# The last MLP chunk interleaved with the weight gradients of all tokens in an adaLN transformer block, with crossbar operands and split weight pools

## The chip, the cores and the metric

One core of one Trainium2 chip. The time is that of one execution on the device in microseconds (us), the median of several. Every kernel ran beside the kernel before on the same chip. A ratio is the mean time of one kernel's runs over the mean of the other's in the same rounds, with a 95% interval, so it is not quite the ratio of the medians quoted beside it. A class of "same" means within 2%.

In the profile's lines PE is the matrix engine (PEld its loading of weights), DVE is VectorE, ACT ScalarE, POOL GpSimd, and SPq SyncE's queue, in which transfers are issued one after the other. A pool is a region of on-chip memory that is opened and closed as a whole.

## The reference, cut to what matters

Forward and all gradients of one block: 2048 tokens, width 512, 32 heads of 16, an MLP of 1792 with squared ReLU, and scale, shift and gate vectors from a condition `c`.

```python
sa, ca, ga, sb, cb, gb = (silu(c) @ w_mod).reshape(6, D)
x1 = x + ga * (softmax_attention(layernorm(x) * (1 + ca) + sa) @ wo)
u  = (layernorm(x1) * (1 + cb) + sb) @ w1 + b1
out = x1 + gb * (relu(u)**2 @ w2 + b2)
# outputs: out, and the gradients of x, wqkv, wo, w1, b1, w2, b2, c, w_mod for a given grad_out
```

The change touches the gradients of w1 (out_4), b1 (out_5), w2 (out_6), b2 (out_7) and of `sb`, `cb`, `gb`. They need the MLP's values of all tokens with tokens on the partitions ("token-major"), while the MLP makes them with features on the partitions: something must transpose.

## The kernel before

It runs four stages: modulation; the attention forward with the MLP of each finished chunk of 512 queries worked in beside it; a weight-gradient stage; the attention backward with the last weight gradients. The weights of the MLP are loaded, scaled and transposed by the crossbar (a DMA that transposes) when the q, k and v projections are done. They lie in one pool, which takes over the memory of the projections' pools:

```python
    if (qc, g, jp) == (1, 0, 0):          # second chunk of queries begins
        bg.drain(); self.close_qkv()      # projections' pools closed
        self.open_mlp(); bg.add(self.gen_weights())
...
def open_mlp(self):
    sb = self.open_pool("mlp", bufs=1, side="right")     # w1, w2, wo, W1mT, W2gbT, wogaT
    self.mk = self.open_pool("mlpk", bufs=1, side="right")
def gen_weights(self):
    nc.sync.dma_start(wo...); nc.sync.dma_start(w1...); nc.sync.dma_start(w2...)
    ... # wo *= gate
    nc.sync.dma_start_transpose(self.wogaT..., wo...)
    ... # w2 *= gate
    nc.sync.dma_start_transpose(self.W2gbT..., w2...)    # 128 x 7168, 1792 KB
```

The same SyncE queue carries, for each piece of 512 tokens of each group of four heads, the store of q or k and a small crossbar transpose:

```python
def gen_fm(self, ps, t, g, s0, eng="vector"):     # one piece of q or k
    ... 4 matmuls -> pt
    ev = eb.tile([P, 512], BF16, name="ev_fm")    # 3 buffers
    nc.vector.tensor_scalar(ev[:], pt[:], bc, None, ALU.add)
    nc.sync.dma_start((self.QTq_d, self.KTq_d)[t][g, :, s0:s0 + 512], ev[:])
    tm = eb.tile([P, 4, 4, 32], BF16, name="ev_tm")
    nc.sync.dma_start_transpose(tm[:]..., ev[:])
```

The weight-gradient stage transposes on PE, block by block, after the last MLP chunk:

```python
for ft in range(FT):                              # 14 blocks of 128 features
    ... # load rT_f, duT_f; square rT_f
    for (srcT, dst, eng) in ((aT_f, a_blk, "act"), (duT_f, du_blk, "dve")):
        ... # 16 PE transposes each, evicted by ACT or DVE
    ... # 16 matmuls -> g2 (w2 gradient), 1 float32 accumulation
    ... # 64 narrow matmuls -> g4 (w1 gradient)
```

The softmax here doesn't subtract the row's maximum and nothing guards it: scores larger than these inputs give would overflow.

Of the kernel before, what the change touches and what calls it, by code (L numbers as in the profile page):

```python
# [8 lines left out]
BF16 = mybir.dt.bfloat16  # L9
# [9 lines left out]
P = 128  # L19
# [53 lines left out]
class K:  # L73
# [29 lines left out]
    def build(self, ctx: ExitStack):  # L103
# [22 lines left out]
        phases = [self.phase0, self.phase_fwd, self.phase45, self.phase5, self.phase6]  # L126
# [136 lines left out]
    def phase_fwd(self):  # L263
# [18 lines left out]
        pup = self.open_pool("fwp", bufs=4)  # L282
        stp = self.open_pool("fwst", bufs=2, space=PSUM)
        accp = self.open_pool("fwacc", bufs=1, space=PSUM)
        self.mps = self.open_pool("mps", bufs=3, space=PSUM)
# [71 lines left out]
        bg.drain()  # L357
        self.close_mlp()
        for name in ("mps", "fwacc", "fwst", "fwp", "fwk", "fw"):
            self.close_pool(name)  # L360

# [151 lines left out]
    def open_mlp(self):  # L513
        nc, io = self.nc, self.io
        D, F, DT, FT, SC, NQ = self.D, self.F, self.DT, self.FT, self.SC, self.NQ
        sb = self.open_pool("mlp", bufs=1, side="right")
        self.mk = self.open_pool("mlpk", bufs=1, side="right")
        self.w1 = sb.tile([P, DT, F], BF16, name="w1")
        self.w2 = sb.tile([P, FT, D], BF16, name="w2")
        self.wo = sb.tile([P, DT, D], BF16, name="wo3")  # L520
        self.W1mT = sb.tile([P, DT, FT, P], BF16, name="W1mT")
        self.W2gbT = sb.tile([P, FT, DT, P], BF16, name="W2gbT")
        self.wogaT = sb.tile([P, DT, DT, P], BF16, name="wogaT")
        self.bias1 = sb.tile([P, FT], F32, name="bias1")
        self.b2gb_b = sb.tile([1, D], BF16, name="b2gb_b")
        self.mhalf = sb.tile([P, 4], F32, name="mhalf")
        nc.vector.memset(self.mhalf[:], -0.5)
        self.db1_part = sb.tile([P, FT, SC], F32, name="db1_part")
        nc.vector.memset(self.db1_part[:], 0.0)
        self.dOpads = [sb.tile([P, NQ, 4, 32], BF16, name=f"dOpad{i}") for i in range(2)]  # L530
        for t in self.dOpads:
            nc.gpsimd.memset(t[:], 0.0)

    def close_mlp(self):
        nc = self.nc
        nc.vector.tensor_reduce(self.db1[:], self.db1_part[:], axis=AX.X, op=ALU.add)
        db1_b = self.mk.tile([P, self.FT], BF16, name="db1_b")
        nc.vector.tensor_copy(db1_b[:], self.db1[:])
        with nc.allow_non_contiguous_dma(reason="column-layout store"):
            nc.sync.dma_start(self.io["out_5"].rearrange("(t p) -> p t", p=P), db1_b[:])  # L540
        self.close_pool("mlpk")
        self.close_pool("mlp")
# [50 lines left out]
    def gen_mlp(self, sc, O_b):  # L593
# [36 lines left out]
        rT = mk.tile([P, FT, 512], BF16, name="rT")  # L630
# [12 lines left out]
        nc.gpsimd.dma_start(self.rT_d.rearrange("ft p s -> p ft s")[:, :, s0:s0 + 512], rT[:])  # L643
        yield ("wait", 1)
        for k in range(4):
# [8 lines left out]
            nc.gpsimd.dma_start(out_v[:, k, :], o[:])  # L654
        duT = mk.tile([P, FT, 512], BF16, name="auT")
# [7 lines left out]
        nc.gpsimd.dma_start(self.duT_d.rearrange("ft p s -> p ft s")[:, :, s0:s0 + 512], duT[:])  # L663
        yield ("wait", 1)
        todo = []
        for k in range(4):
# [18 lines left out]
            todo.append((k, dxT))  # L685
            if k:
# [66 lines left out]

    def gen_4b(self, sb2, lb, ob, accps, ps, trps):
        tc, nc, pp, io = self.tc, self.nc, self.pp, self.io
        S, D, F, H, ST, DT, FT, SC = self.S, self.D, self.F, self.H, self.ST, self.DT, self.FT, self.SC
        g_v = io["grad_out"][0].rearrange("(st p) d -> p st d", p=P)
        xh2_v = self.xhat2_d.rearrange("(st p) d -> p st d", p=P)
        db1 = self.db1
        g_tm = sb2.tile([P, ST, D], BF16, name="g_tm")  # L760
        nc.sync.dma_start(g_tm[:], g_v)
        xh2 = sb2.tile([P, ST, D], BF16, name="xh2")
        nc.gpsimd.dma_start(xh2[:], xh2_v)
        w1_v = io["B_w1"].rearrange("(kt p) f -> p kt f", p=P)
        b2_b = sb2.tile([P, D], BF16, name="b2_b")
        nc.sync.dma_start(b2_b[:], io["B_b2"].rearrange("(o d) -> o d", o=1).to_broadcast([P, D]))
        csg_ps = ps.tile([P, 512], F32, name="g2ps")
        for st in range(ST):
            nc.tensor.matmul(csg_ps[:, :D], lhsT=self.ones_b[:], rhs=g_tm[:, st, :], start=(st == 0), stop=(st == ST - 1))
        csg = sb2.tile([P, D], F32, name="csg")  # L770
        nc.vector.tensor_copy(csg[:], csg_ps[:, :D])
        db2 = sb2.tile([P, D], BF16, name="db2")
        nc.vector.tensor_tensor(db2[:], csg[:], self.mod_row(5), ALU.mult)
        nc.sync.dma_start(io["out_7"].rearrange("(o d) -> o d", o=1), db2[0:1, :])
        db1_bc = sb2.tile([P, F], F32, name="db1_bc")
        acc_cb = sb2.tile([P, DT, P], F32, name="acc_cb")
        nc.vector.memset(acc_cb[:], 0.0)
        opcb_b = self.opcbT[:].unsqueeze(2).to_broadcast([P, DT, P])
        sbT_b = self.mod_col(3).unsqueeze(2).to_broadcast([P, DT, P])
        dgb_ps = accps.tile([P, 512], F32, name="dgb_ps")  # L780
        dw1_v = io["out_4"].rearrange("(kt p) f -> p kt f", p=P)
        yield
        for ft in range(FT):
            rT_f = lb.tile([P, S], BF16, name="rT_f")
            duT_f = lb.tile([P, S], BF16, name="duT_f")
            nc.sync.dma_start(rT_f[:], self.rT_d[ft])
            nc.gpsimd.dma_start(duT_f[:], self.duT_d[ft])
            w2_blk = lb.tile([P, D], BF16, name="w2_blk")
            w1_blk = lb.tile([P, DT, P], BF16, name="w1_blk")
            with nc.allow_non_contiguous_dma(reason="256B runs"):  # L790
                nc.sync.dma_start(w1_blk[:], w1_v[:, :, ft * P:(ft + 1) * P])
            nc.gpsimd.dma_start(w2_blk[:], io["B_w2"][ft * P:(ft + 1) * P, :])
            aT_f = rT_f
            nc.scalar.activation(aT_f[:], rT_f[:], ACT.Square)
            a_blk = lb.tile([P, ST, P], BF16, name="a_blk")
            du_blk = lb.tile([P, ST, P], BF16, name="du_blk")
            for (srcT, dst, eng) in ((aT_f, a_blk, "act"), (duT_f, du_blk, "dve")):
                for s0 in range(0, ST, 8):
                    n = min(8, ST - s0)
                    pt = trps.tile([P, 8 * P], BF16, name="trps")  # L800
                    for k in range(n):
                        nc.tensor.transpose(pt[:, k * P:(k + 1) * P], srcT[:, (s0 + k) * P:(s0 + k + 1) * P], self.ident[:])
                    dv = dst[:, s0:s0 + n, :].rearrange("p s f -> p (s f)")
                    if eng == "act":
                        nc.scalar.copy(dv, pt[:, :n * P])
                    else:
                        nc.vector.tensor_copy(dv, pt[:, :n * P])
            g2 = ps.tile([P, 512], F32, name="g2ps")
            for st in range(ST):
                nc.tensor.matmul(g2[:, :D], lhsT=a_blk[:, st, :], rhs=g_tm[:, st, :], start=(st == 0), stop=(st == ST - 1))  # L810
            dw2 = ob.tile([P, D], BF16, name="dw2")
            nc.vector.tensor_tensor(dw2[:], g2[:, :D], self.mod_row(5), ALU.mult)
            nc.sync.dma_start(io["out_6"][ft * P:(ft + 1) * P, :], dw2[:])
            tmp = ob.tile([P, D], F32, name="g2w2")
            nc.vector.tensor_tensor(tmp[:], g2[:, :D], w2_blk[:], ALU.mult)
            nc.tensor.matmul(dgb_ps[:, :D], lhsT=self.ones_f[:], rhs=tmp[:], start=(ft == 0), stop=(ft == FT - 1))
            yield
            g4 = ps.tile([P, DT, P], F32, name="g4ps")
            for kt in range(DT):
                for st in range(ST):  # L820
                    nc.tensor.matmul(g4[:, kt, :], lhsT=xh2[:, st, kt * P:(kt + 1) * P], rhs=du_blk[:, st, :],
                                     start=(st == 0), stop=(st == ST - 1))
            diag = ob.tile([P, P], F32, name="diag")
            nc.vector.tensor_scalar(diag[:], self.ident_f[:], db1[:, ft:ft + 1], None, ALU.mult)
            csb_ps = ps.tile([P, P], F32, name="csbps")
            nc.tensor.matmul(csb_ps[:], lhsT=self.ones_f[:], rhs=diag[:], start=True, stop=True)
            csb = db1_bc[:, ft * P:(ft + 1) * P]
# [473 lines left out]
```

## Time and profile before

| what | us |
|---|---|
| median (3 runs, 3136.89 to 3143.05) | 3139.95 |
| profiled execution | 3141.7 |
| attention forward, first to last exponential | 104.3 to 1131.5 |
| from there to the first score matmul of the backward, the stretch that the change rebuilds | 326.3 |
| attention backward and the rest | 1683.9 |

The prediction below shows the stretch.

```profile
127.76 0.53 SPq L445 DMA_DIRECT2D QTq_d<-ev_fm  x1
...
136.57 0.52 SPq L445 DMA_DIRECT2D QTq_d<-ev_fm  x1
...
140.28 0.51 SPq L445 DMA_DIRECT2D QTq_d<-ev_fm  x1
```

The q pieces of the second head group come every few us.

### The profile page before, as it was taken

What the parts mean: (1) busy time and instruction counts of PE and PEld (TensorE: products, weight loads), DVE (VectorE), ACT (ScalarE), POOL (GpSimd) and SP (SyncE); (2) the same over time, 40 slices, a digit from 0 to 9 for tenths busy, and PEclk for the clock granted to TensorE, in tenths of its full rate; (3) what the DMA queues carried; (4) which work ended last, traced back from release to release, by engine and by line L of the source; (5) the groups of instructions that cost most, each with busy time, mean ns of one, the idle gap of its engine ahead of it and who ended that gap; (6) DMA issues with size and microseconds to landing.
All of it is one profiled execution on the core that took longest, in us unless ns stands there. A gap on an engine that the chain in (4) does not pass through costs nothing. (4 is left out here: it accounts for less than half of the span.)

```text
span 3141.7 us, 73207 instructions
## 1 busy us (share of the span) xinstructions
PE 2765.5 (88%) x30278; PEld 1440.6 (46%) x30788; DVE 1866.1 (59%) x2741; ACT 2274.9 (72%) x3325; POOL 322.8 (10%) x569
## 2 busy tenths in 40 slices
PE   4799899889989966688999999999999999999796
PEld 1355455445545532464444444444444444444343
DVE  5222231331332244546888888888887888888565
ACT  3599999889989941234777777777777777777533
POOL 2433111211221122300000000000000000000000
PEclk7899999999999988899999999999999999999998
DMA  3855620431251155646999999999999999999942
GB/s 132 190 127 133 144 68 26 122 80 56 74 121 54 53 127 117 212 134 143 193 191 201 188 203 192 196 196 188 207 191 203 190 191 204 188 191 181 228 133 66
DMA packets 1276003, 473.93 MB, mean 151 GB/s; under 512 B 1205970, under 2 KB 1235796, under 8 KB 1275668
## 3 DMA queue, kind: packets, MB, share of 16 engines
q1 hardware_dynamic: 1245892, 376.78, 63.2%
q0 software_dynamic: 29248, 90.86, 9.7%
q8 instruction: 241, 3.95, 0.5%
q10 hardware_dynamic: 528, 1.57, 0.1%
q14 instruction: 94, 0.77, 0.1%
HBM read 103.68 MB, written 67.64 MB: 55 GB/s over the span
## 5 line engine op out<-in xcount | busy, mean ns | idle before, releaser
L1018 ACT ACTIVATE pu<-st 128x512 bf16<-128x512 f32 x2048 | 1133.1, 597 | 322.3 <-PE st L1016 307.0
L1023 DVE TENSOR_TENSOR ds<-dp,pu 128x1024 bf16<-128x1024 f32 x1024 | 1209.0, 1220 | 242.1 <-ACT pu L1018 234.1
L348 ACT ACTIVATE pu<-st 128x1024 bf16<-128x1024 f32 x1024 | 959.6, 1041 | 68.7 <-PE st L345 57.7
L1016 PE MATMUL st<-KTm,QTq 128*128 128x512 bf16 x2048 | 780.6, 381 | 14.9 <-ACT pu L1018 9.5
L964 PEld LDWEIGHTS <-dsT 128*128 128x128 bf16 x8192 | 488.0, 96 | 497.0 <-DMA dsT<-ds 23.9
L1019 PE MATMUL dp<-VTm,dOTq 128*128 128x512 bf16 x1779 | 675.5, 380 | 7.9 <-DVE ds L1023 5.9
L345 PE MATMUL st<-QTm,KTq 128*128 128x512 bf16 x1938 | 592.9, 382 | 48.9 <-issue 13.8
L964 PE MATMUL accq<-Kg,dsT 128*128 128x16 bf16 x8192 | 493.9, 170 | 32.2 <-DMA dsT<-ds 17.8
L315 PEld LDWEIGHTS <-pu 128*128 128x128 bf16 x8192 | 355.3, 96 | 318.0 <-issue 86.5
L315 PE MATMUL accbank<-Vaug,pu 128*128 128x17 bf16 x8192 | 359.1, 171 | 64.6 <-DVE accbank L311 57.7
L944 PE MATMUL acckv<-ds,Qg 128*16 128x512 bf16 x2048 | 309.9, 383 | 0.8 <-DVE ds L1023 0.7
L944 PE MATMUL acckv<-pu,dOg 128*16 128x512 bf16 x2048 | 309.9, 383 | 0.0
L1016 PEld LDWEIGHTS <-QTq 128*128 128x128 bf16 x2048 | 196.2, 96 | 225.8 <-issue 221.2
L345 PEld LDWEIGHTS <-KTq 128*128 128x128 bf16 x2048 | 193.0, 96 | 205.0 <-issue 147.2
L1019 PEld LDWEIGHTS <-dOTq 128*128 128x128 bf16 x2048 | 197.6, 96 | 36.6 <-DVE ds L1023 16.2
L1195 POOL DMA_DIRECT2D wmod<-in_w_mod_dram x6 | 4.6, 762 | 1563.8 <-DMA dsT<-ds 1527.7
L444 DVE TENSOR_SCALAR ev_fm<-pps,bcol 128x512 bf16<-128x512 f32 x60 | 45.0, 751 | 152.9 <-PE pps L436 87.8
L296 POOL DMA_DIRECT2D QTm<-QTq_d x128 | 64.8, 509 | 444.1 <-PE st L345 400.4
L322 DVE RECIPROCAL rl<-accbank 128x4 f32<-128x4 f32 x128 | 23.0, 179 | 136.6 <-PE accbank L315 136.2
L661 DVE SCALAR_TENSOR_TENSOR auT<-pps,rT 128x512 bf16<-128x512 f32 x56 | 38.7, 692 | 95.6 <-PE pps L659 83.2
L635 PE MATMUL pps<-fT,w 128*128 128x512 bf16 x224 | 72.9, 384 | 20.7 <-DMA fT<-xh 20.7
L641 DVE TENSOR_SCALAR rT<-pps,bias 128x512 bf16<-128x512 f32 x42 | 31.5, 751 | 93.9 <-PE pps L635 93.8
(277 smaller groups left out, 2183.5 us busy)
## 6 DMA issues: line engine op xcount, KB each, us to landing
KTq<-KTq_d POOLq DMA_DIRECT2D x32, 512.0 KB, 3.9
rT_d<-rT POOLq DMA_DIRECT2D x4, 1792.0 KB, 8.5
duT_d<-auT POOLq DMA_DIRECT2D x4, 1792.0 KB, 8.6
duT_f<-duT_d POOLq DMA_DIRECT2D x14, 512.0 KB, 3.7
rT_f<-rT_d SPq DMA_DIRECT2D x14, 512.0 KB, 4.0
QTq_d<-ev_fm SPq DMA_DIRECT2D x32, 128.0 KB, 2.2
QTm<-QTq_d POOLq DMA_DIRECT2D x128, 32.0 KB, 2.0
KTq_d<-ev_fm SPq DMA_DIRECT2D x32, 128.0 KB, 2.0
```

The source lines that it names most:

```text
L296: nc.gpsimd.dma_start(QTm[j][32 * j:32 * j + 32, :], self.QTq_d[g, 32 * j:32 * j + 32, 512 * qc:512 * (qc + 1)])
L315: nc.tensor.matmul(acc[:, a, sub, :], lhsT=pu[:, a, sub * P:(sub + 1) * P], rhs=Vaug[:, kb, h, :], start=False, stop=False, skip_group_che ...
L345: nc.tensor.matmul(stt[:, a, :], lhsT=KT[:, kb * P:(kb + 1) * P], rhs=QTm[2 * jp + a][:], start=True, stop=True)
L348: nc.scalar.activation(pu[:], stt[:], ACT.Exp, scale=self.scale)
L444: nc.vector.tensor_scalar(ev[:], pt[:], bc, None, ALU.add)
L635: nc.tensor.matmul(pt[:], lhsT=self.w1[:, kt, ft * P:(ft + 1) * P], rhs=xhT[:, :, kt, :], start=(kt == 0), stop=(kt == DT - 1))
L944: nc.tensor.matmul(acckv[r:r + DH, :], lhsT=T[n][:, ib, col:col + DH], rhs=src[:, a, :], start=(ib == 0), stop=(ib == ST - 1))
L964: nc.tensor.matmul(accq[:, ib, a, :], lhsT=dsT[:, (i * 2 + a) * 4 + sub, :], rhs=T["K"][:, 4 * c + sub, col:col + DH], start=(c == 0 and i ...
L1016: nc.tensor.matmul(stt[:], lhsT=T["QT"][:, q], rhs=masked["KT"][2 * jp + a][:, c0:c0 + 512], start=True, stop=True)
L1018: nc.scalar.activation(pu[:, a, :], stt[:], ACT.Exp, scale=self.scale)
L1019: nc.tensor.matmul(dp[:, a, :], lhsT=T["dOT"][:, q], rhs=masked["VT"][2 * jp + a][:, c0:c0 + 512], start=True, stop=True)
L1023: nc.vector.tensor_tensor(dsg[:, i], dp[:], pu[:], ALU.mult)
```

## The change

Its intent: PE's waits in the last MLP chunk (layer norm, transposes, layer-norm backward) are filled with weight-gradient matmuls; their operands come token-major straight from the crossbar, so that PE's 448 transposes and their evictions go; and the weight pool is cut in four so that the last chunk can free it part by part.

```diff
-        sb = self.open_pool("mlp", bufs=1, side="right")
         self.mk = self.open_pool("mlpk", bufs=1, side="right")
+        sb = self.open_pool("mlp0", bufs=1, side="right")      # W1mT, wogaT, small tiles
+        sb = self.open_pool("mlp_da", bufs=1, side="right")    # W2gbT, rT
+        sb = self.open_pool("mlp_f", bufs=1, side="right")     # w2
+        sb = self.open_pool("mlp_u", bufs=1, side="right")     # w1, wo
...
+    def last_mlp(self, bg):
+        nc.gpsimd.dma_start(g_tm[:], io["grad_out"]...)
+        fill = Background()
+        fill.add(self.gen_csg(dw, g_tm))                        # 16 column-sum matmuls of grad_out
+        while True:
+            r = bg.next()                                       # the MLP, up to its next wait
+            ...
+            if r[0] == "wait":
+                for _ in range(4 * r[1]):
+                    if fill.next() is None: break
+            elif r[0] == "u":                                   # first MLP matmuls done
+                self.close_pool("mlp_u")
+                fill.add(self.gen_dw2(...))
+            elif r[0] == "f":  self.close_pool("mlp_f")
+            elif r[0] == "da":
+                self.close_pool("mlp_da")
+                ... # db1; out_5 stored in 2-byte pieces on GpSimd's queue
+                fill.add(self.gen_dw1(...))
+        fill.drain()
...
+    def gen_dw2(self, sb, g_tm):
+            nc.sync.dma_start_transpose(r[:], self.rT_d[ft])    # a_blk, 3 buffers
+            nc.scalar.activation(a[:], a[:], ACT.Square)
+            ... # 16 matmuls; GpSimd adds up dgb_acc; one float32 matmul at the end
+    def gen_dw1(self, sb, xh2):
+            nc.sync.dma_start_transpose(r[:], self.duT_d[ft])   # du_blk, 3 buffers
+            ... # 64 matmuls; after the last block:
+        for kt in range(DT):
+            w1k = sb.tile([P, F], BF16, name="w1k", bufs=1)
+            nc.gpsimd.dma_start(w1k[:], w1_v[:, kt, :])
+            ... # 4 products each for dsb_col
-    def gen_4b(...)                                             # the old stage, with its PE transposes
```

Other edits: the pool of the projections in PSUM (the memory that matmuls write to) is opened ahead of the attention's, `rT` moves into the pool of W2gbT, in the w1 gradient two small operations of each block go from VectorE to GpSimd, and most loads and stores of the gradients go from SyncE's queue to GpSimd's.

## The prediction

> **What bounds the kernel now.** I first read busy time by slice on the page, then cut out the stretch that the change touches: from the last attention-forward exponential (line L348, at 1131.5 us) to the first score matmul of the attention backward (L1016, 1457.85 us). Everything before and after keeps its instructions, so only this stretch can move. Busy time of each engine in four parts of it (columns: window, length, busy us and instruction count per engine, granted clock, DMA share, GB/s):
>
> ```profile
> 1133.00:1168.70 35.70, 7.12 (x20) 2.35 (x20) 14.28 (x37) 0.00 (x0) 8.66 (x14) 0.61 0.74 172
> 1168.70:1252.70 84.00, 59.42 (x241) 24.33 (x244) 36.88 (x102) 17.59 (x30) 15.49 (x25) 0.85 0.49 101
> 1252.70:1290.20 37.50, 12.41 (x43) 8.37 (x45) 17.97 (x31) 7.33 (x16) 18.79 (x18) 0.54 0.83 258
> 1290.20:1457.80 167.60, 144.18 (x1583) 102.72 (x1595) 92.26 (x164) 51.26 (x40) 15.21 (x26) 1.00 0.44 129
> ```
>
> The reader should see 324.8 us, of which PE works 223. The first three rows, 157 us, hold the last chunk's MLP and the loading of the weight-gradient stage, with PE busy half the time. The fourth is the weight gradients, 14 blocks, bound by PE at full clock. Next, PE's own waits there:
>
> ```profile
> PE pps L720 <- DMA dxT<-dxb: 26.9, 4, 17.2
> PE trps L802 <- ACT a_blk L805: 16.3, 14, 1.4
> PE pps L635 <- DMA fT<-xh: 16.1, 1, 16.1
> PE csbps L826 <- DVE dsb_part L846: 14.3, 1, 14.3
> PE csbps L826 <- DVE diag L824: 10.3, 1, 10.3
> PE pps L616 <- DMA fT<-O_b: 9.8, 1, 9.8
> ```
>
> These are chains of dependence (layer norm, crossbar transpose, load), not throughput: filling them with independent matmuls is what the change is for. Then the groups of the stretch, to price each piece (busy us, mean ns of one):
>
> ```profile
> L821 PE MATMUL g4ps<-du_blk,xh 128*128 128x128 bf16 x896 | 54.6, 219 | 0.0
> L810 PE MATMUL g2ps<-g_tm,a_blk 128*128 128x512 bf16 x210 | 52.2, 379 | 0.7
> L805 ACT COPY a_blk<-trps 128x1024 bf16<-128x1024 bf16 x28 | 28.3, 1012 | 65.6 <-PE trps L802 65.6
> L794 ACT ACTIVATE rT_f<-rT_f 128x2048 bf16<-128x2048 bf16 x14 | 26.6, 1910 | 37.9 <-DMA rT_f<-rT_d 37.9
> L802 PE MATMUL trps<-ident,rT_f 128*128 128x128 bf16 x224 | 17.0, 219 | 16.3 <-ACT a_blk L805 16.3
> L802 PE MATMUL trps<-ident,duT_f 128*128 128x128 bf16 x224 | 17.0, 218 | 1.3 <-DVE du_blk L807 1.0
> L816 PE MATMUL dgb_ps<-g2w,ones_f 128*128 128x512 f32 x28 | 15.8, 645 | 0.6
> L852 DVE SCALAR_TENSOR_TENSOR junk<-db_bc,w1k 128x512 f32<-128x512 f32 x12 | 7.8, 686 | 0.0
> ```
>
> A mean of 219 ns is latency; start to start, the timeline has 56 matmuls of 512 columns in 12.1 us (0.216 each), and the 64 narrow ones of a block in 3.77 us. Last, transfers (issue to landing, us), for the chains that remain:
>
> ```profile
> rT_d<-rT POOLq DMA_DIRECT2D x1, 1792.0 KB, 9.1
> duT_d<-auT POOLq DMA_DIRECT2D x1, 1792.0 KB, 20.7
> fT<-xh SPq DMA_TRANSPOSE x1, 6.3
> out_dram<-db_b SPq DMA_DIRECT2D x1, 3.5 KB, 15.7
> ```
>
> **What the Trainium skill says.** "DMA: Bandwidth & Descriptors", section "Latency and other measured facts", gives 261 GB/s for one kernel's crossbar transposes; 0.5 MB would take 2 us. Here a 0.5 MB one lands 6.3 us (from SBUF) or 7.9 us (grad_out from DRAM) after issue, and in attention backward 1 MB is sustained every 5.8 us; I use these: about 3 us of throughput, 6.5 to 8 of latency. The same page, "Specifications", says that transfers under 512 B are read-modify-written; the 3.5 KB store of out_5 in 2-byte pieces takes 15.7 us, and dx and dxT transfers beside it 15 and 16. Its section "Issuing engines are not separate DMA queues" says all issuers share 16 engines, which agrees. "TensorE: Matmul & The Clock Gate", Part 1, says that an idle window of about 3.4 us halves the clock; the trace grants 0.50 between 1220 and 1232, and cold 512-column matmuls take 0.43 each instead of 0.22.
>
> **The change, part by part.** I walked PE's order in the built changed kernel, which is fixed by hand there, and looked at which instruction each wait names; durations are the trace's.
>
> Removed. The 448 PE transposes (14 x 32; eight take 0.45 us, so 25 us), their ACT evictions (28 us) and DVE evictions (19 us), 14 accumulating float32 matmul pairs (0.96 each, 13.5 us; one pair stays, the adding goes to GpSimd) and the 16 us that PE waited for evictions. The block period falls from 11.57 us (1340.77 to 1352.33) to PE's 3.45 (16 wide matmuls) plus 3.77 plus 0.63 (float32 bias broadcast) = 7.85 us if operands arrive in time. The 37.5 us of loading between the stages mostly vanishes, as g_tm loads right after the attention.
>
> Added: 28 crossbar transposes of 0.5 MB from DRAM, which cost PE nothing but have to keep up, and new places where PE's fixed order waits. Step by step from 1133 us:
>
> 1. Output projection and layer norm: 35.7 us before. Now 16 column-sum matmuls stand ahead and need g_tm, 2 MB issued near 1141.5 and landing, as an estimate from the 9 to 14 us of other 2 MB transfers, near 1153. That delays the chain by 5: 40.7 us. The 16 us wait for fT<-xh stays: no other fill exists yet.
> 2. First MLP matmuls, 56: 13.4 us, as before.
> 3. New stall. Four weight-gradient matmuls stand before the second MLP matmuls, and need rT of the last chunk: store 9.1, transpose 7, square 1.9, semaphores and issue about 1, four cold matmuls 2: 21 us against none before.
> 4. Second MLP matmuls, W2gbT matmuls, first block of the input gradient: 29.0 us (1182.15 to 1211.1) plus four fills 0.9.
> 5. The four layer-norm-backward chains: 41.6 us before. Now 88 fill matmuls (19 us) lie between, but three du_blk transposes sit in the same in-order queue ahead of dxT of tile 1, waiting for duT to land, while the 2-byte store still clogs the engines. I estimate 54.5 us.
> 6. The remaining 132 fill matmuls, 8.25 blocks. Three buffers circulate: load 7 + square 1.9 + matmuls 3.45 + 0.5, over 3, is 4.3 us, over PE's 3.45: 35.5 us.
> 7. DVE product, GpSimd add and the one float32 reduction, in PE's way: 4.3 us.
> 8. The w1 gradient: 14 x 4.40 = 61.6 us, PE bound; the ring would allow (7 + 4.4 + 0.3)/3 = 3.9.
> 9. New tail. Before, the 16 products for dsb_col (L852) were done by 1308.8 under other work. Now they stand after the last block, with one w1k buffer: 4 products 2.5 us, then three times load 4.1 + 2.5 + 0.3; with the last block's DVE work 4.5 before it, 27.5. The backward's first QTq load waits on the reduction that ends this, as its memory was these pools'. Then 3.1 us from load to first matmul: 30.5 us, where before it was 4.5 (1453.3 to 1457.85).
>
> Sum: 40.7 + 13.4 + 21 + 29.9 + 54.5 + 35.5 + 4.3 + 61.6 + 30.5 = 291.4 us against 324.8: 33.4 us less. 3139.95 - 33.4 is about 3106 us. Weights also load earlier, during the forward's first stretch, which is as likely to cost a few us in transfers as to gain any.
>
> **Rivals.** (a) The interleave works better than my step 5 and 6: PE never waits in them. PE has 88 + 132 fills, 42 gradient and 16 projection matmuls, 278 x 0.216 = 60 us in place of 90; total 3076, just over 2% faster. For it: DMA share is 0.44 in the gradient stage before; against it: dxT alone waited 26.9 us on PE, and its queue gets longer. (b) The crossbar from DRAM becomes the bound, 5 to 6 us a block: grad_out's transposes hold the queue 6 us each. Then steps 6 and 8 take 47 and 77 us instead of 35.5 and 61.6: 3133. Against it: 1 MB in 5.8 us is sustained in the backward. (c) The tail does not stall, because the backward starts under it: 26 us less, 3080. Against it: the waits of the QTq load name the last reduction, and on DVE the 16 products stand before the first ds. (d) Early weight transposes delay the forward's q and k for the second group: up to 10 us lost, 3116.
>
> **Range and chances.** The fixed parts (steps 2, 4, 8 and the tail) are good to 5 us; steps 3 and 5 to 7 carry plus or minus 20 together, skewed down a little by (a) and up by (b). So 3106, 8 in 10 within 3078 to 3136. The line of 2% is 3077: faster 0.11, within 0.85, slower 0.04.
>
> **What would show it.** Right: no PE transposes in the stretch; a PE wait near 20 us for a_blk's square just before the second MLP matmuls; block periods of about 4.3 and 4.4 us; about 25 us with PE idle before the first L1059 matmul, with DVE waiting three times for w1k; that matmul near 1424 us. Wrong: a w1-gradient period above 5 us with waits on du_blk (rival b); a first backward matmul within 10 us of the last gradient matmul (c); the forward's last exponential ending later than 1132 by over 5 us (d); or a changed length of the backward, which I take as equal.

## More of the kernel before

The part of the forward that turned out to matter is its first 100 us, in which the projections of the other seven head groups run beside the exponentials. Busy time of each engine there (window, length, busy us and count of PE, PEld, DVE, ACT, POOL, then granted clock, DMA share, GB/s):

```profile
104.00:204.00 100.00, 88.35 (x1023) 47.99 (x1041) 24.49 (x52) 88.97 (x96) 40.69 (x87) 0.95 0.70 164
```

ACT has 96 instructions in these 100 us, all but one of them exponentials, and PE is as busy: how far the forward has come can be read off that count.

Between 104 and 160 us the queue's issues add up to 44.5 of 56 us, most of it small transposes: the queue has little to spare.

## The result

The changed kernel took 3134.64 us (median of 4 runs, 3133.26 to 3142.91) against 3141.5 in the same rounds: ratio 0.9985, 95% interval 0.9963 to 1.0007. A second set of rounds, on another occasion, gave 3140.72 against 3140.18, ratio 1.0000 (0.9976 to 1.0024). So by these two measurements the change is worth between nothing and 7 us, where 33 were forecast.

The four stages of the stretch after the change, from the last P·V matmul of the forward at 1150.4 us to the first score matmul of the backward (columns as above):

```profile
1150.40:1194.80 44.40, 10.71 (x37) 3.90 (x36) 14.77 (x38) 0.59 (x1) 10.36 (x16) 0.63 0.71 186
1194.80:1255.00 60.20, 43.03 (x176) 17.76 (x177) 17.60 (x43) 15.35 (x17) 6.52 (x10) 0.82 0.37 107
1255.00:1319.80 64.80, 40.46 (x162) 16.75 (x161) 28.84 (x70) 13.62 (x19) 25.98 (x40) 0.79 1.04 176
1319.80:1452.10 132.30, 87.29 (x1059) 68.03 (x1057) 70.02 (x124) 19.01 (x22) 85.03 (x94) 0.88 0.71 151
```

PE's work fell from 223 to 181 us, as was meant, but the stretch only from 324.8 to 301.7: PE now stands still for 120 us of it, before for 102. PE's waits there (who waits, for what: us in total, times, longest):

```profile
PE st L1059 <- DMA QTq<-QTq_d: 29.1, 1, 29.1
PE dps L615 <- ACT a_blk L610: 27.8, 8, 17.2
PE pps L880 <- DMA dxT<-dxb: 26.0, 3, 18.9
PE dps L584 <- DMA g_tm<-in_grad_out_dram: 17.4, 1, 17.4
...
PE dps L626 <- POOL dgb_acc L622: 6.2, 1, 6.2
```

All but the third are new or grown: fills that wait for their own operands (L615, L584), the tail (L1059, 4.5 us before) and the GpSimd reduction (L626). The two large groups of matmuls are what they were, with the transposes gone:

```profile
L664 PE MATMUL dps<-du_blk,xh 128*128 128x128 bf16 x896 | 53.7, 222 | 0.0
...
L615 PE MATMUL dps<-g_tm,a_blk 128*128 128x512 bf16 x224 | 51.8, 384 | 27.8 <-ACT a_blk L610 27.8
```

And the stretch starts later. The last forward exponential is at 1149.0 us, not 1131.5. The loss is made early: the points at which each pair of heads begins (its accumulator is cleared) lie 5.2 us later than before for the second pair, 17.5 for the fifth, 19.6 for the sixth, and nearly constant from there to the end. The first 100 us after the change, same columns:

```profile
104.00:204.00 100.00, 78.87 (x818) 39.99 (x819) 27.54 (x55) 71.48 (x75) 34.69 (x73) 0.85 0.89 192
```

75 instructions on ACT instead of 96, 21 exponentials or about 21 us lost; the transfers busier, the clock lower. SyncE's queue (start, duration of the issue, what), where before the q pieces came at 127.8, 136.6 and 140.3:

```profile
128.22 1.37 SPq L445 DMA_DIRECT2D QTq_d<-ev_fm  x1
...
133.31 14.29 SPq L731 DMA_TRANSPOSE W2gbT<-w  x1
147.65 0.58 SPq L445 DMA_DIRECT2D QTq_d<-ev_fm  x1
```

The transpose of w2 stands there for 14.3 us; in the kernel before it came at 332 us and took 9.26. Why it moved: by my reading of the pools' layout, the old pool overlapped the projections' memory and had to wait for its release, while of the four new pools those of w1, w2, wo and W2gbT lie outside that memory, so that nothing holds their loads and transposes back. No run shows the addresses; that cutting the pool moves the loads is shown by e3. In SyncE's order in the built program the weight loads moved from 152nd to 26th, the large transpose from 156th to 45th. What the other engines waited for between 104 and 215 us, in the kernel before and then in the changed one:

```profile
DVE ev_fm L444 <- DMA ev_tm<-ev_fm: 19.1, 6, 6.1
...
ACT pu L348 <- PE st L345: 11.0, 10, 5.6
```

```profile
POOL ev_tmc L449 <- DMA ev_tm<-ev_fm: 44.9, 12, 13.1
...
DVE ev_fm L444 <- DMA ev_tm<-ev_fm: 29.6, 5, 13.4
ACT pu L348 <- PE st L345: 26.0, 15, 8.5
```

GpSimd's waits add up to the same as before (44.3 us in 21 waits), but come in fewer and longer ones; those of VectorE and ScalarE grow. The small q and k transposes are late, so VectorE cannot reuse their buffers, and what stands behind it in VectorE's order (clearing the accumulators) and behind the k load (score matmuls) makes PE and then ACT wait.

So there are three accounts to settle: the forward's 17.5 us; the new waits in the stretch; and the worth of the interleaving itself.

### The profile page after: what moved, and what is told of

Read it like the earlier page. It is cut to its first block, busy times and chain, and to the rows that moved or that the text cites. A ratio compares the mean times of both kernels' runs of the same rounds, so it can differ in the third digit from the quotient of the medians. Undisturbed runs are those within 1.5% of the kernel's fastest.

```text
span 3131.5 us, 72698 instructions
## 1 busy us (share of the span) xinstructions
PE 2760.6 (88%) x30314; PEld 1410.0 (45%) x30314; DVE 1835.4 (59%) x2683; ACT 2247.8 (72%) x3298; POOL 393.4 (13%) x647
## 5 line engine op out<-in xcount | busy, mean ns | idle before, releaser
L1059 PE MATMUL st<-KTm,QTq 128*128 128x512 bf16 x2048 | 779.4, 381 | 39.0 <-DMA QTq<-QTq_d 29.1
L1062 PE MATMUL dp<-VTm,dOTq 128*128 128x512 bf16 x2048 | 775.5, 379 | 7.1 <-DVE ds L1066 5.8
L345 PE MATMUL st<-QTm,KTq 128*128 128x512 bf16 x2048 | 621.0, 385 | 44.1 <-issue 16.3
L1007 PE MATMUL accq<-Kg,dsT 128*128 128x16 bf16 x8192 | 493.5, 170 | 17.2 <-DMA dsT<-ds 17.1
L315 PEld LDWEIGHTS <-pu 128*128 128x128 bf16 x8192 | 356.2, 96 | 326.3 <-issue 96.4
L1059 PEld LDWEIGHTS <-QTq 128*128 128x128 bf16 x2048 | 196.1, 96 | 249.3 <-issue 244.6
L436 PE MATMUL pps<-xhat1T,wpad 128*128 128x512 bf16 x256 | 92.1, 396 | 0.0
```

What stands on the lines that cost most here:

```text
L315: nc.tensor.matmul(acc[:, a, sub, :], lhsT=pu[:, a, sub * P:(sub + 1) * P], rhs=Vaug[:, kb, h, :], start=False, stop=False, skip_group_che ...
L345: nc.tensor.matmul(stt[:, a, :], lhsT=KT[:, kb * P:(kb + 1) * P], rhs=QTm[2 * jp + a][:], start=True, stop=True)
L436: nc.tensor.matmul(pt[:], lhsT=self.wpads[t][:, kt, g, :], rhs=self.xhat1T[:, kt, s0:s0 + 512], start=(kt == 0), stop=(kt == DT - 1))
L1007: nc.tensor.matmul(accq[:, ib, a, :], lhsT=dsT[:, (i * 2 + a) * 4 + sub, :], rhs=T["K"][:, 4 * c + sub, col:col + DH], start=(c == 0 and i ...
L1059: nc.tensor.matmul(stt[:], lhsT=T["QT"][:, q], rhs=masked["KT"][2 * jp + a][:, c0:c0 + 512], start=True, stop=True)
L1062: nc.tensor.matmul(dp[:, a, :], lhsT=T["dOT"][:, q], rhs=masked["VT"][2 * jp + a][:, c0:c0 + 512], start=True, stop=True)
```

## The experiments

All gave correct results. "Forward end" is the last forward exponential, "stretch" the time from it to the first backward score matmul, "rest" what follows; these three are of the one profiled execution.

| run | median us | ratio to before (95%) | forward end | stretch | rest |
|---|---|---|---|---|---|
| before | 3139.95 | 1 | 1131.5 | 326.3 | 1683.9 |
| changed | 3134.64 | 0.9985 (0.9963-1.0007) | 1149.0 | 303.1 | 1679.4 |
| e1 late weights | 3120.89 | 0.9928 (0.9912-0.9944) | 1131.3 | 309.9 | 1675.3 |
| e2 late transposes | 3123.16 | 0.9931 (0.9916-0.9946) | 1136.8 | 306.3 | 1676.8 |
| e3 before, split pools | 3150.39 | 1.0018 (1.0003-1.0032) | 1151.0 | 319.4 | 1678.4 |
| e4 no fill | 3121.71 | 0.9930 (0.9914-0.9947) | 1146.0 | 295.2 | 1671.9 |
| e5 sums later | 3112.91 | 0.9907 (0.9890-0.9924) | 1148.9 | 285.9 | 1674.2 |
| e6 tail in loop | 3130.32 | 0.9956 (0.9941-0.9971) | 1146.1 | 303.8 | 1674.9 |
| e7 out_5 by rows | 3123.16 | 0.9935 (0.9919-0.9952) | 1148.5 | 291.8 | 1678.0 |
| e8 all mended | 3064.30 | 0.9750 (0.9736-0.9765) | 1131.4 | 253.6 | 1677.9 |
| e9 + products on ACT | 3060.87 | 0.9744 (0.9731-0.9756) | 1134.5 | 247.7 | 1674.6 |
| e10 + sums in the wait | 3060.54 | 0.9737 (0.9723-0.9750) | 1134.1 | 247.7 | 1679.5 |
| e11 partly mended, no fill | 3087.48 | 0.9831 (0.9817-0.9845) | 1131.7 | 280.6 | 1673.9 |
| e12 before, split, late | 3134.31 | 0.9976 (0.9965-0.9988) | 1132.2 | 321.7 | 1675.6 |
| e13 transpose in pieces | 3141.60 | 1.0003 (0.9978-1.0027) | 1152.5 | 311.7 | 1679.6 |
| e14 changed again | 3140.72 | 1.0000 (0.9976-1.0024) | 1147.7 | 316.3 | 1679.3 |

The two rows of the changed kernel are the measure of chance: one profile's stretch differs from the other's by 13 us with the same instructions, most of it in the layer-norm-backward and w2-gradient stages, while the forward ends within 1.3 us (within 3 us over the six profiles with that forward unchanged: e4 to e7 and these two). The rest varies by 12 us over all kernels without a cause that any run shows. So I read sizes from the ratios, and mechanisms from the waits.

### e1: weights held back

```diff
     def gen_weights(self):
+        for t in (wo, w1, w2):
+            nc.vector.tensor_copy(t[0:1, 0, 0:1], self.rl[0:1, 0, 24:25])   # softmax sums of head 24
         nc.sync.dma_start(wo[:], ...)
```

> The changed kernel, but each of the three MLP weight tiles gets one element written from the softmax sums of head 24 of the first query chunk before it is loaded, so the loads and the weight transposes go back to the place in SyncE's order that they have in the kernel before (152nd to 156th instead of 26th to 45th); results stay right. Theory Q (the early loads and transposes sit among the q and k pieces of the first quarter of the forward and hold up SyncE's in-order queue): the last forward exponential ends near 1133 us again instead of 1150, and the whole time falls by 15 to 18 us, to about 3118. Rival P (the forward lost its 17.5 us to another part of the change, such as the PSUM pools in another order, which this kernel keeps): the forward still ends near 1150 and the time stays at 3134.

```profile
104.00:204.00 100.00, 88.80 (x1021) 48.20 (x1039) 24.40 (x52) 89.02 (x96) 40.68 (x87) 0.95 0.72 164
```

96 instructions on ACT again, and the forward ends at 1131.3. The time falls to 3120.89: 13.8 us less in medians, 0.57 to 0.72% less in ratios (against the two of the changed kernel), which is 18 to 23 us. Theory Q holds and rival P falls, as the PSUM pools stayed as changed. SyncE's order in the forward was that of the kernel before, but for two small bias loads, which stay behind the weights here.

### e2: loads early, transposes late

```diff
+        for i in range(2):      # the gate rows, rewritten with their own values once head 24 is done
+            nc.vector.scalar_tensor_tensor(self.mod_25[:, i, 0:1], self.rl[:, 0, 24:25], 0.0,
+                                           self.mod_25[:, i, 0:1], ALU.mult, ALU.add)
         for kt in range(DT):
             nc.vector.tensor_tensor(wo[:, kt, :], wo[:, kt, :], self.mod_row(2), ALU.mult)
```

> The changed kernel with the three weight loads (4 MB) as early as it has them, but the two weight transposes back at their old place (155th and 156th in SyncE's order): their operand products wait for the softmax sums of head 24 through an element of the modulation row that is written with its own value. If the transposes, which take 14.3 and 2.75 us to issue in the queue, do the harm: the forward ends at 1133 to 1137 and the time is within 4 us of that of the kernel with late weights. If the loads' bytes do it: the forward still ends at 1146 to 1150. In between, both share: I expect the transposes to be about 13 of the 17.5 us and the loads about 4, as the first exponential starts 3.3 us later in the changed kernel than before.

```profile
104.00:204.00 100.00, 85.26 (x972) 46.17 (x991) 23.00 (x51) 85.32 (x91) 39.54 (x84) 0.94 0.83 190
```

91 instructions on ACT; the forward ends at 1136.8. Of the 17.7 us between the changed kernel and e1, the late transposes make 12.2 and the loads 5.5, each of one profile and good to some 3 us; the times of e1 and e2 do not tell them apart (2.3 us in medians, intervals overlap). 4.4 of those 5.5 are lost before the first exponential (108.9 us against 104.5 in e1), while the loads run beside the projections' first transfers. As expected. The edit also holds back VectorE's products that feed the transposes, some 12 us of VectorE up to 129.4 us in the changed kernel. The traces put the loss behind them: the second pair's accumulator is cleared at 126.9 us in the changed kernel and 126.5 in e2, the third's at 154.7 and 143.8, with VectorE's wait of 13.4 us for a small transpose between.

### e3: the reverse, the kernel before with split pools

```diff
-        sb = self.open_pool("mlp", bufs=1, side="right")
         self.mk = self.open_pool("mlpk", bufs=1, side="right")
+        sb = self.open_pool("mlp", bufs=1, side="right")       # W1mT, wogaT, small tiles
+        da = self.open_pool("mlp_da", bufs=1, side="right")    # W2gbT
+        f = self.open_pool("mlp_f", bufs=1, side="right")      # w2
+        u = self.open_pool("mlp_u", bufs=1, side="right")      # w1, wo
```

> The kernel before with nothing changed but the right-hand weight pool cut into the four pools of the changed kernel, opened in its order and all closed together as before: its SyncE order in the forward becomes that of the changed kernel (loads 26th to 30th, transposes 39th and 45th). Theory Q: the forward ends near 1150 and the kernel is 15 to 18 us slower than before, about 3157. Rival P (PSUM pool order): the same as before, 3140.

The forward ends at 1151.0, 19.5 us later than before: this part of the change alone makes the whole loss of the forward. But the kernel is only 0.18% slower (7 us in medians), not 0.5%: both expectations miss. Some is given back in the stretch, and the profile says where from. The load of grad_out for the gradient stage (duration of the issue, then the start), before and in e3:

```profile
L761 SPq DMA_DIRECT2D g_tm<-in_grad_out_dram x1: 389/389/389, 1265.9 to 1265.9; - x1
```

```profile
L764 SPq DMA_DIRECT2D g_tm<-in_grad_out_dram x1: 392/392/392, 1201.8 to 1201.8; - x1
```

That is 134 us after the last exponential before, and 51 us after it in e3 (again 51 in e12): with the pool in pieces the load need not wait for the last user of all of it, even though all pieces are closed together. PE's two waits of 14.3 and 10.3 us at the start of the gradient stage are gone in e3, though waits for dxT grow from 26.9 to 36.1 us. So the split pools do two things at once, one at each end of their life.

### e12: both ends together, in the kernel before

e3 with the edit of e1.

> The kernel before with the split weight pools and the late weights, nothing else. With split pools alone the forward ended 19.5 us later, but grad_out's load was issued 51 us after the last exponential instead of 134, PE's waits of 14.3 and 10.3 us for the loading of the gradient stage were gone, and only 7 us of loss remained. If both effects are independent, the late weights give back 17 to 19.5 us: 7 to 12 us faster than before, about 3132. If the earlier loads were only possible in the shadow of the later forward: the same as before.

3134.31 us, ratio 0.9976, 7.5 us faster than before (0.24% of 3143), with the forward's end at 1132.2 and the stretch 4.6 us shorter. As far as this shows, the two effects add up. Note that two small edits to the old kernel do as well as the whole change did.

### e13 and e14: one large transpose in 14 pieces, and the control

```diff
         for ft in range(FT):
             nc.vector.tensor_tensor(w2[:, ft, :], w2[:, ft, :], self.mod_row(5), ALU.mult)
+            nc.sync.dma_start_transpose(self.W2gbT[:, ft], w2[:, ft, :])
-        nc.sync.dma_start_transpose(self.W2gbT[:]..., w2[:]...)
```

> The changed kernel with its one early crossbar transpose of w2 (1.79 MB, 14.3 us in SyncE's queue) cut into 14 of 128 KB; they stay early, but in the order of SyncE ten of them alternate with the q and k pieces of the second and third head group, in groups of at most six. Bytes and time are the same, only the block in the queue is broken up. Theory Q1 (the head of the queue is what delays the q and k pieces): the forward ends 6 to 10 us earlier than the changed kernel's 1149, near 1141, and the time falls by as much. Rival Q2 (the transposed bytes themselves compete with the small transposes and loads): the forward ends within 3 us of 1149 as before.

> The changed kernel itself once more, on the same chip and in the same rounds, as the control of the run before and to see how far the forward's end and the backward's length vary from one execution to the next: time 3131 to 3138, last forward exponential at 1146 to 1151 (two kernels with the same forward gave 1146.0 and 1148.9).

The forward ends at 1152.5 in e13, at 1147.7 in its control: breaking up the block does not help. Theory Q1 in its simple form, one long instruction at the head of the queue, is refuted. The 14 pieces took 23 us of SyncE's queue in all, in runs of up to 8.4 us, and the queue had no such time to give: its issues between 104 and 160 us add up to 44.5 us before, 41.8 in e1, 47.6 in the changed kernel and 49.4 in e13, and the q piece that came at 147.65 comes at 146.05. Whether it is the time in the queue or the bytes behind it (DMA share 0.84 in e13, 0.89 in the changed kernel) stays open: every run that took one away took the other away too. What is shown is that the transposes' presence in that stretch, with the products ahead of them (e2), costs about 12 us, in one piece or in 14.

### e4: the interleaving taken out alone

```diff
-                for _ in range(4 * r[1]):
+                for _ in range(0):
```

> The changed kernel with the interleaving taken out alone: no weight-gradient matmul is put into the last MLP's waits, all of them run when the MLP is done; crossbar operands, pools and tail stay. The 92 w2-gradient and 16 column-sum matmuls that now lie in the MLP's waits are 23 us of PE at 0.216 us each, but they also bring two waits of PE, 17.4 us for grad_out and 17.2 us for the first squared block, of which the layer-norm chain hides part of the first. Theory F (the interleave as placed pays its own gain back): within 8 us of the changed kernel on either side. Rival (the interleave earns what it hides, the stalls would be there anyway): 18 to 25 us slower.

Both miss: the kernel without interleaving is faster, 3121.71 us against 3134.64, ratio 0.9930 against 0.9985 and 1.0000. In the profile the first squared block and grad_out are no longer waited for in the MLP's path: the first MLP matmul comes 42.0 us after the last exponential instead of 45.8, the second MLP matmuls 14.0 us after that instead of 33.5. As placed, the interleave cost more than it hid. Two of the fills make the difference, as e5 shows next: with these moved, the interleaved kernel is 8.8 us ahead of this one in medians.

### e5: the column sums as the first safe fill

```diff
         fill = Background()
-        fill.add(self.gen_csg(dw, g_tm))
...
             elif r[0] == "u":
                 self.close_pool("mlp_u")
+                fill.add(self.gen_csg(dw, g_tm))
                 fill.add(self.gen_dw2(self.open_pool("dw2", bufs=2), g_tm))
```

> The changed kernel with the 16 column-sum matmuls of grad_out moved in the fill order alone: from ahead of the output projection to ahead of the first w2-gradient block, so that the four fills that stand before the second MLP matmuls are column sums, whose operand has long landed, instead of matmuls that need the first squared block. Theory S (the placement of two fills makes the stalls of 17.4 us for grad_out and 17.2 us for the squared block): the second stall goes wholly, of the first about 7 us (the layer-norm chain behind it starts that much earlier; without fills it started 16 us after the last exponential instead of 28), so the stretch falls by 20 to 25 us and the time to about 3112. Rival (the waits only move: the squared block is then waited for at the next fill, and the projection waits for its own transposes): within 6 us of the changed kernel.

```profile
PE dps L615 <- ACT a_blk L610: 11.5, 4, 4.4
```

The 17.2 us wait for the squared block is gone (from 27.8 in all to 11.5, longest 4.4), grad_out is waited for no more, and the time falls by 0.8 to 0.9% to 3112.91. From the last exponential to the first MLP matmul it takes 41.0 us instead of 45.8, and the second MLP matmuls follow 15.8 us later instead of 33.5: 22 us, as theory S said. Moving sixteen matmuls to a place where their operand has landed is worth more than the whole change brought.

### e6: the tail's products inside the blocks

```diff
+            for kt in range(DT):       # in each w1 block, on the w1_blk that is there
+                nc.vector.scalar_tensor_tensor(junk[:], csb, 1.0, w1_blk[:, kt, :], ALU.mult, ALU.mult,
+                                               accum_out=dsb_part[:, kt, ft:ft + 1])
-        for kt in range(DT):
-            w1k = ...; nc.gpsimd.dma_start(w1k[:], w1_v[:, kt, :])
-            ... # four products of 512 columns
```

> The changed kernel with the 16 products for dsb_col after the last block (with four loads through one buffer) replaced by four small products in each of the 14 blocks, on the w1 block that is loaded there anyway; results the same up to rounding. Theory T (the backward's first load waits on the last reduction, and the 29 us of PE idle at the end are the serial loads and products): the wait before the first backward matmul falls from 29 us to 8 to 12, the time by about 19 us to 3115, as far as four more VectorE products in a block of 3.9 us do not make VectorE the bound of the w1 gradient. Rival (that load waits for the stores and the other readers of this memory, or for the queue): a wait of 25 us or more stays.

The last wait fell from 29.1 to 18.2 us, not to 10, and the time by 4 us in medians, 0.3 to 0.4% (9 to 14 us) in ratios, where 19 were expected. The w1-gradient blocks of the changed kernel and of e6 (columns as above; the third busy time is VectorE's):

```profile
1367.30:1422.50 55.20, 55.18 (x922) 54.81 (x921) 38.22 (x53) 3.46 (x13) 41.99 (x49) 0.97 0.91 163
```

```profile
1371.30:1430.00 58.70, 55.26 (x923) 54.17 (x921) 53.95 (x136) 3.45 (x13) 39.61 (x45) 0.99 0.81 148
```

VectorE went from 38 to 54 us of a stage of 58.7: it became the bound, slowed the blocks by 3.5 us and was still working when PE had finished. The gain was turned into a new wait.

### e7: out_5 by rows

```diff
-                    nc.gpsimd.dma_start(io["out_5"].rearrange("(t p) -> p t", p=P), db1_b[:])   # 2-byte pieces
+                nc.tensor.transpose(r5[0:FT, 0:P], db1[:], self.ident_f[:])      # in the first w1 block
+                nc.vector.tensor_copy(db1_r[:], r5[0:FT, 0:P])
+                nc.gpsimd.dma_start(io["out_5"].rearrange("(t p) -> t p", p=P), db1_r[:])
```

> The changed kernel with the 3.5 KB store of out_5 in 2-byte pieces replaced by a PE transpose of the 128x14 values and one store of 14 rows of 256 bytes, in the first w1 block. Theory C (the 2-byte store, 24 us from issue to landing, clogs the engines beside the layer-norm-backward chains): the three PE waits for dxT, 26 us, fall to 10 to 14 and the time by 8 to 14 us. Rival (the dxT transposes stand in SyncE's order behind du_blk transposes that wait for duT to land): the waits stay above 20 us and the time changes by less than 5 us.

```profile
PE pps L882 <- DMA dxT<-dxb: 12.0, 4, 5.3
```

The waits for dxT fall from 26.0 to 12.0 us and the time by 0.5 to 0.65%, to 3123.16. Theory C holds. The rival has a part in it: the three du_blk transposes that stand in SyncE's queue ahead of the second dxT took 18.6 us of it in the changed kernel and 12.0 here, so some of the gain comes through them. A store of 3.5 KB that took 23.9 us to land cost about ten microseconds or more of the kernel's time; as 14 rows of 256 bytes it lands in 4.8. The edit also moves the store to a later place, and no run separates the new shape from the new place.

### e8: all mends together

e1, e5, e6, e7, and the last float32 reduction (L626) moved behind the third w1 block, which was not run alone.

> All mends together: late weights, column sums later, the dsb products inside the blocks, out_5 by rows, and the last float32 reduction of the w2 gradient placed after the third w1 block instead of ahead of the first. If they add up: 17 (forward) + 20 (fills) + 19 (tail) + 8 (out_5) + 5 (reduction) = 69 us less than the changed kernel, about 3066, 2.4% under the kernel before. If the gains overlap (the same transfers wait elsewhere): 3075 to 3095.

3064.30 us, 2.5% faster than before, and 70 less than the changed kernel's 3134.64, where 69 were expected. That the sum fits so well is chance in part: the tail brought less than expected, so other terms brought more. PE's waits that lead in the stretch now:

```profile
PE pps L794 <- DMA fT<-xh: 19.5, 1, 19.5
PE dp L1069 <- DMA dOTq<-dOTq_d: 17.9, 1, 17.9
```

The first is the layer-norm chain with nothing to fill it, the second the tail with VectorE behind.

### e11: two of the mends, without the interleaving

As built, this is not what its expectation says. It has the edits of e1, e6 and e4, but not e8's store of out_5 by rows (the store took 24.8 us to land here) nor the moved reduction. Where the column sums stand makes no difference without fills.

> All mends of the eighth run, without the interleaving: every weight-gradient matmul after the MLP. What the interleave is worth when its fills never wait for a late operand: it moves about 108 matmuls of 0.216 us under the waits, 23 us, so 20 to 25 us slower than with all mends (3085 to 3090). If the fills mostly delay the chains between them, less than 8 us.

3087.48 us, 23 more than e8, and so inside the expected range, but by luck: the 23 us hold the interleave and two mends, of which e7 alone brought 11.5 us in medians in the changed kernel. A cleaner pair is e4 and e5. They differ in the interleave alone, and neither has the two stalls: 3121.71 and 3112.91 us, 8.8 us in medians, 0.23% (7 us) in ratios, whose intervals overlap a little. So the interleave costs more than it hides when the first fills' operands are not there (e4), and seems to earn 7 to 9 us when they are. What it is worth with all mends stays open: no run takes it out of e8 alone.

### e9 and e10: two steps further

e9 makes the products with the shift and scale columns on ScalarE, four activations with a per-partition scale each; e10 also puts the column sums between the output projection and the first MLP matmuls.

```diff
-            nc.vector.tensor_tensor(t1[:], csb.unsqueeze(1).to_broadcast([P, DT, P]), sbT_b, ALU.mult)
+            for kt in range(DT):
+                nc.scalar.activation(t1[:, kt, :], csb_ps[:, :P], ACT.Copy, scale=self.mod_col(3)[:, kt:kt + 1])
-            nc.vector.tensor_tensor(t2[:], g4[:], opcb_b, ALU.mult)
+            for kt in range(DT):
+                nc.scalar.activation(t2[:, kt, :], g4[:, kt, :], ACT.Copy, scale=self.opcbT[:, kt:kt + 1])
```

```diff
             if r[0] == "wait":
+                if first:                       # the wait ahead of the projection: no fill, queue the sums
+                    first = False; fill.add(self.gen_csg(dw, g_tm)); continue
+                if skip:                        # the wait behind the first MLP matmuls: no fill
+                    skip = False; continue
```

> All mends, and two of VectorE's products in each w1 block (times the shift column, times the scale column) made by ScalarE in four pieces each, as ScalarE is idle there. With all mends VectorE needs 4.7 us a block (four products of 0.68, four small ones of 0.29 with 0.08 for their sums, one of them stretched to 1.35 beside GpSimd's adding) against PE's 3.9, ends 12.7 us after the last gradient matmul, and the backward waits 17.9 us. Theory V (VectorE became the bound when the products moved into the loop): without 1.36 us of it a block is PE's again, the lag falls to 4 to 6 us, and the time falls by 8 to 12 us to about 3054. Rival (the wait is for the last store of the w1 gradient, not for VectorE): it stays above 14 us, and the time falls by less than 4.

> As the run before (products on ScalarE), with the 16 column-sum matmuls placed between the output projection and the first MLP matmuls, where PE waits 19.5 us for the layer norm and grad_out has landed (13.8 us after its issue at 1141.6), and no fill at the wait behind the first MLP matmuls. The 16 then cost nothing: 16 x 0.216 = 3.5 us less, up to 7 if they ran on the slow clock, so 3047 to 3052 if the run before gives 3054. If the sums still hold up the MLP, 5 us more than the run before.

e9 brought 3.4 us in medians (3060.87; the intervals overlap), not 8 to 12; the last wait is 15.0 us instead of 17.9. By both numbers this is what the rival foretold, that the wait is for the last store of the w1 gradient. The trace has VectorE and the store in one chain: VectorE's last product for that store ends at 1373.9 us, 7 us after the last gradient matmul; the store is issued at 1374.2; SyncE's queue, whose wait the profile puts down to the store (`SPq L1034 <- DMA out_dram<-dw: 22.3`), issues the backward's first load at 1377.1; the matmul follows at 1381.85. VectorE itself ends 10 us after the last gradient matmul. One reason shows in the timeline of e9 (start, duration): the first small product of a block runs beside GpSimd's adding, the second does not.

```profile
1366.40 1.53 DVE L697 SCALAR_TENSOR_TENSOR junk_sb<-db_bc,w_blk 128x128 f32<-128x128 f32 x1 [0.43 <-DMA w_blk<-in_B_w_dram]
1366.49 1.27 POOL L695 TENSOR_TENSOR acc_cb<-acc_cb,t 128x512 f32<-128x512 f32 x1
...
1367.97 0.29 DVE L697 SCALAR_TENSOR_TENSOR junk_sb<-db_bc,w_blk 128x128 f32<-128x128 f32 x1
```

1.53 us against 0.29 for the same instruction. The Trainium skill, "SBUF — State Buffer", section "SBUF: two separate sides", says that VectorE instructions with two SBUF inputs and a GpSimd instruction that reads SBUF take turns on a pair of ports, each blocking the other for a whole instruction; the trace agrees, with 1.24 us added beside an adding of 1.27. No run takes the adding away, so its share of the lag is not measured.

e10, expected at 3047 to 3052 if e9 gave 3054, changes nothing further (3060.54; the intervals overlap). In its profile the sums do run inside the layer-norm wait, which shrinks from 20.6 to 16.9 us, and the layer-norm-backward stage is 3 us longer; with one profile of each that difference is not settled. These two are the fastest kernels, 2.6% faster than before.

## Why the prediction was wrong, point by point

The class was right, and the time of the first rounds lay just inside the range (3134.64, with 3136 as its end), that of the second outside it (3140.72); but the gain was forecast as 33 us and is 0 to 7. By the first profile: 33.4 forecast; the stretch gave 23.1 (324.8 to 301.7), the forward took 17.4 (its last P·V matmul at 1150.4 instead of 1133.0), the rest gave 4.4 that I had not counted and that may be chance: 10.1, the difference of the two profiled spans (3141.7 and 3131.5).

**The step that failed** is the one that is not in the sum: "Everything before and after keeps its instructions, so only this stretch can move", and with it rival (d), "Early weight transposes delay the forward's q and k for the second group: up to 10 us lost". The instructions were kept, their order was not. I had seen that the weights load earlier and called it "as likely to cost a few us in transfers as to gain any": the term was put at 0 and measured 17.7 (e1), about 12 of it from the transposes and 5.5 from the loads (e2). The forward's first stretch is where SyncE's queue and the transfers have least room, and 17 us of transposes were added to it.

The steps of the stretch, in us, from the first profile:

| step | forecast | measured |
|---|---|---|
| 1 projection and layer norm | 40.7 | 44.4 |
| 2 first MLP matmuls | 13.4 | 14.6 |
| 3 wait for the first squared block | 21 | 18.9 |
| 4 second MLP matmuls and on | 29.9 | 30.8 |
| 5 layer-norm-backward chains | 54.5 | 60.7 |
| 6 rest of the w2 gradient | 35.5 | 39.4 |
| 7 last reduction | 4.3 | 8.1 |
| 8 w1 gradient | 61.6 | 55.7 |
| 9 tail | 30.5 | 29.1 |
| sum | 291.4 | 301.7 |

- Steps 3 and 9 were right in kind, place and size, and the experiments confirm their causes: e5 removes the first, e6 shortens the second. (The terms of step 9 as listed add up to 30.8, not 30.5.) Rival (c), no tail, falls.
- Step 1 had the right wait (grad_out), but the load landed 13.2 us after an issue at 1158.8. e5 shows that it held up the chain.
- Step 5 was short by 6 us, and in e14 steps 5 and 6 together were another 10 longer. The cause that I named, the 2-byte store, is shown by e7; I gave it too little. Step 6 was short by 4 us: 4.8 us a block where 4.3 were forecast, with 9.7 us of PE's waits for squared blocks, whose squaring waited 24.0 us for the crossbar. Rival (a), no waits in 5 and 6, falls; rival (b) has a part in step 6.
- Step 8 was too long: a block takes 3.85 us, as the 64 narrow matmuls take 3.57 and the float32 pair 0.28. Rival (b), the crossbar as the bound, falls for this stage: PE's weight loads wait 0.2 us for du_blk in all.
- Step 7 was short by 4 us; GpSimd's adding takes 1.28 us a block and lagged.
- The interleaving: I expected it to earn, with stalls as its price. e4 shows that the price was higher than the earnings; e4 against e5 puts the earnings at 7 to 9 us once these two stalls are gone. The stalls were in my own list, so the mend could have been named at once.

## What to carry to other kernels

When a pool is split, or memory moves for any reason, ask which instructions were held back by the old overlap, and look at every queue's new order over the whole kernel, not only at the stretch that the change was made for. A filler is only free when its operand has landed: put first what needs the oldest data, and check each new filler's own load against the time at which PE reaches it. Taking a wait away shows the next one (e6 made VectorE the bound), so mend one at a time and then all together.

## What the Trainium skill lacked or had wrong

- "DMA: Bandwidth & Descriptors" has bandwidths for crossbar transposes and, in its part on trn3, sequencer cycles for some transposes of "previous generations", but no time that one of a given size keeps its issuing queue on this chip. The runs show 1.2 us for 128 KB, and for 1792 KB 9.26 us in a quieter stretch (the kernel before, DMA share 0.43 from 320 to 360 us) and 14.29 in a busy one (the changed kernel, 0.89 from 104 to 204 us). There it landed 16.3 us after issue: 113 GB/s (1.835 million bytes over 16.3 us), far below the 261 the page gives for one kernel. In e8, where it stands at 338.7 us, it landed after 11.6 us, 158 GB/s.
- The same page says that transfers under 512 bytes are read-modify-written, but not what that does to others: with 3.5 KB in 2-byte pieces, which took 23.9 us to land, PE's waits for the dxT transfers were 26.0 us, and 12.0 with the store reshaped and moved (e7).
- No page has a word on how the memory of pools decides the order in which transfers are issued; here that was worth 17.7 us of the forward (e1).
